# Fetching k and v as 112 rows and 16 more, and interleaving q, k and v with the weights

## The chip, the cores and the metric

The kernel runs on one core of a Trainium2 chip. A core has a matrix engine (TensorE, PE in the profile), a vector engine (VectorE, DVE), a scalar engine (ScalarE, ACT), GpSimd (POOL) and a sync engine (SyncE, SP) whose queue issues nearly all transfers here. The data is moved by 16 DMA engines. On-chip memory (SBUF) has 128 partitions; matmuls write to PSUM banks. The metric is the device time of one execution in microseconds, the median over several executions. Before the change it is 926.72 us (926.64 to 927.29 over 3 runs).

## What is computed

The kernel joins a linear attention block to a two-matrix feed-forward block. For each of 8 batches and 8 heads, with 576 positions and head size 64:

```python
kv = np.einsum('bhsd,bhse->bhde', k, v)
out = np.einsum('bhsd,bhde->bhse', q, kv)
rms = np.sqrt(np.mean(out * out, axis=-1, keepdims=True) + 1e-06)
x = (out / rms * g_norm)              # then (B,H,S,D) -> (B*S, H*D) = 4608 x 512
h = x @ w_in                          # 512 x 2048, float64 weights
sp = np.maximum(h, 0.0) + np.log1p(np.exp(-np.abs(h)))
y = (h * erf(sp)) @ w_out             # 2048 x 512
```

The feed-forward weights come as 64-bit floats, all else as 32-bit floats. What matters for the change is the first line. kv is a sum over the 576 positions, and TensorE sums over partitions, so the positions of k and v are spread over partitions in several chunks. In which chunk and partition a position lies makes no difference to the sum, as long as k and v agree.

## The kernel before

**Tiling.** The 4608 tokens are handled as nine groups of 512: the first 512 positions of each of the 8 batches (T = 0 to 7), and a ninth group of the 64 last positions of every batch (`x_last`). Heads are taken in pairs, four pairs (p = 0 to 3) to a batch. Pair i = 4T + p has one q tile, one k tile and one v tile in SBUF; the pools hold two of each kind (`bufs=2`).

**Stages.** Batch 0's attention is done alone at the start (to about 28 us) while the raw 64-bit weights begin to arrive. Groups 0 and 1 then run their feed-forward in a loop over n (32 steps of some 7 us, to about 250 us), the attention of the next batch running beside them in pieces. In group 0 the raw weights (`w_raw`, fetched by `load_w`, L213 and L218) are turned into 32-bit ones. In group 1 the 32-bit weights are cut into upper and lower parts: ACT writes the upper part (L596), VectorE the lower (L599, L602), and SP stores the three forms to DRAM (`w_in<-w_new`, `w_out<-w_new`, L672, 768 KB each). From group 2 on, the main loop runs steps m of about 23.8 us: four `hidden` products (x by w_in), and four `result` products (gates by w_out), each of 12 matmuls at L634. In every step all eight weight parts are read back from DRAM (`load_parts`, L773, 768 KB each), and one head pair of the next batch's attention is worked.

**One head pair of batches 1 to 7.** `load_pair(i)` fetches k and v of the pair two ahead, and `load_q` its q. `visit` applies kv to q, and forms the kv of the next pair (`kv_products`, L449, or L357 for the very first). `turn` transposes the next pair's q on VectorE (L318).

**How k and v lie.** For batches 1 to 7 the 576 positions are cut into C = 5 chunks. `rows, rest = divmod(S, C)` gives 115 rows and 1 over: partition r holds positions 5r to 5r+4 of each head, 1280 contiguous bytes, for r below 115 (L141), and the last position goes to partition 115, chunk 0, in a transfer of its own (L146, 0.5 KB). Batch 0 has 6 chunks of 96 rows and nothing over.

**How q lies.** Each q tile is fetched by eight transfers (L162) of 32 partitions each, in runs of 128 bytes.

**Order of the transfers.** There is no planner; the order is that of the program text. SP issues its transfers in that order. One waits, and all behind it, until its tile is free and until the transfer eight before it on SP has landed, since the transfers signal eight semaphores in turn. In a main-loop step, `fetch(place)` is called at eight places (0 to 3 after the four `hidden` products, 4 to 7 after the four `result` products) and issues weights by the list

```python
    FETCH = ("", "in", "in", "out", "in", "out", "in", "out out")
```

The attention's pieces are run at `places = (0, 2, 3, 5, 6, 8)`; in batches 3 to 7 the third piece, at place 3, holds `loads` and `turn`, so all twelve transfers of a pair (two for k, two for v, eight for q) are issued there in a row. In group 0 and 1's loop `loads` follows `visit`. The two first pairs of batch 1 are special: their k and v are requested in batch 0's loop (`i == 1`), the q of the first after that loop (`load_q(NP)`) and the q of the second at step n = 1.

Of the kernel before, what the change touches and what calls it, by code (L numbers as in the profile page):

```python
# [57 lines left out]
SQ = 32  # L58
# [3 lines left out]
def kernel(  # L62
# [10 lines left out]
    nc = tc.nc  # L73
    P = 128
    B, H, S, D = q.shape
# [4 lines left out]
    NP = H // 2  # L80
# [30 lines left out]
    exp_ln_table()  # L111


    q_sb, k_sb, v_sb = {}, {}, {}


    q_last = early.tile([P, 2, 2, D], FP32, name="q_last", bufs=1)
# [1 line left out]
    def chunks(T):  # L119

        return 6 if T == 0 else 5

    def load_pair(i, turned=True):
        T, p = divmod(i, NP)
        if T >= B:
            return
        pool = early if i in (2, 3) else kvp
        side = nc.scalar if i < 3 else nc.sync
        if T == 0:
            t = pool.tile([P, G if pool is early else S], FP32, name="q_sb", tag="q")  # L130
            t = q_sb[T, p] = t[:, 0:G].rearrange("p (j h d) -> p j h d", j=J, h=2)
            nc.sync.dma_start(
                out=t, in_=q[T, 2 * p : 2 * p + 2, 0:G, :].rearrange("h (p j) d -> p j h d", j=J)
            )
        for name, got, src in (("k", k_sb, k), ("v", v_sb, v)):
            C = chunks(T)
            rows, rest = divmod(S, C)
            assert rest < 2
            t = got[T, p] = pool.tile([rows + rest, 2, C, D], FP32, name=f"{name}_sb", tag=name)
            heads = src[T, 2 * p : 2 * p + 2]  # L140
            side.dma_start(  # L141
                out=t[:rows].rearrange("r h c d -> r h (c d)"),
                in_=heads[:, : S - rest].rearrange("h (r c) d -> r h (c d)", c=C),
            )
            if rest:
                side.dma_start(  # L146
                    out=t[rows:, :, 0], in_=heads[:, S - rest :].rearrange("h r d -> r h d")
                )
        if T > 0 and turned:
            load_q(i)  # L150

    def load_q(i):


        T, p = divmod(i, NP)
        t = q_sb[T, p] = kvp.tile([P, S], FP32, name="q_sb", tag="q")
        for n in range(P // SQ):
            h, w = divmod(n, D // SQ)
            to = t[n * SQ : n * SQ + SQ].rearrange("a (j b) -> a j b", b=SQ)
            for head, js in ((1 - h, slice(0, G // 2 // SQ)), (h, slice(G // 2 // SQ, S // SQ))):  # L160
                src = q[T, 2 * p + head, :, w * SQ : w * SQ + SQ]
                nc.sync.dma_start(  # L162
                    out=to[:, js], in_=src.rearrange("(j a) b -> a j b", a=SQ)[:, js]
                )

    def load_last(p):
        nc.sync.dma_start(
# [106 lines left out]
    def w_next(what):  # L274
        i = w_at[what]
        if i < len(w_order):
            w_at[what] = i + 1
            {"load": load_w, "split": w_split, "join": w_join}[what](*w_order[i][1:])
# [41 lines left out]
    def kv_products(T, p, at, crossed):  # L320


        ks, vs = (x.pop((T, p)) for x in (k_sb, v_sb))
        C = chunks(T)
        for c in range(C):
            for r in range(2):
                rows = (slice(0, D), slice(D, S // C + (c < S % C)))[r]
                for i in range(2):
                    yield partial(
                        nc.tensor.matmul,  # L330
                        at[rows_of[i], 1 - (r ^ i) if crossed else r, kv_cols],
                        lhsT=ks[rows, i, c],
                        rhs=vs[rows, i, c],
                        start=(c == 0),
                        stop=(c == C - 1),
                    )
# [29 lines left out]
    def attention(T, p, pools=None, in_parts=False):  # L366
# [31 lines left out]
        def products():  # L398

            kv_ps = st["kv"] = bank("kv_ps")  # L400
            ks, vs, qs = (x.pop((T, p)) for x in (k_sb, v_sb, q_sb))
            C = chunks(T)
            for c in range(C):
                rows = slice(0, S // C + (c < S % C))
                for i in range(2):
                    s = rows_of[i]
                    nc.tensor.matmul(
                        kv_ps[s, s],
                        lhsT=ks[rows, i, c],
                        rhs=vs[rows, i, c],  # L410
                        start=(c == 0),
                        stop=(c == C - 1),
                    )
            if p % 2 == 0:
                nc.tensor.transpose(kv_ps[:, q_tail], q_last[:, p // 2], ident)
            st["qT"] = square_tile("qT")
            for s in rows_of:
                nc.vector.tensor_copy(out=bd[s, s], in_=kv_ps[s, s])
            if p % 2 == 0:
                tails[T] = attp.tile([P, G], FP32, name="qT_last", tag="sq_lo")[:, 0:P]  # L420
                nc.vector.tensor_copy(out=tails[T], in_=kv_ps[:, q_tail])
            st["tail"] = tails[T][:, p % 2 * R : p % 2 * R + R]
            qt_ps = bank("qt_ps")
            for j in range(J):
                nc.tensor.transpose(qt_ps[:, j * P : j * P + P], qs[:, j], ident)
            nc.scalar.copy(st["qT"], qt_ps)
# [123 lines left out]
            split_lower()  # L550

        def loads():
            load_pair(T * NP + p + 2)

        if T == 0:
            return products, apply, halve, mean, norm
# [4 lines left out]
        first_ = (partial(prepare, T, p),) if (T, p) == (1, 0) else ()  # L561
        then_ = partial(turn, *then)
        if apart:
            pieces = (first_, (visit, halve, keep_tail), (loads, then_))
            return (*(partial(chain, *group) for group in pieces), mean, norm, *after)
        pieces = (first_, (visit, loads), (halve, keep_tail) if halves else (keep_tail,))
        return (*(partial(chain, *group) for group in pieces), mean, partial(chain, norm, then_), *after)
# [176 lines left out]
    for i in range(NP + 3):  # L744
        for piece, p in ((0, i), (1, i - 1), (4, i - 3), (3, i - 2)):
            if 0 <= p < NP:
                first[p][piece]()
        if i == 1:
            for _ in range(RAW - 2):
                w_next("load")  # L750
            load_pair(NP, turned=False)
            load_pair(NP + 1, turned=False)
        for what in w_rounds.get(i, ()):
            w_next(what)


    w_late.append(True)
    load_q(NP)
    first_batch, batches = FIRST * NB, NG * NB
    w_seq = {  # L760
        which: [(which, f) for _ in range(NG - FIRST) for f in range(FC)] for which in ("in", "out")
# [3 lines left out]
    def load_parts(which, n):  # L765


        pool = w_out_p if which == "out" and len(w_seq["out"]) > BATCH else w_in_p
        for _ in range(n):
            if w_seq[which]:  # L770
                key = w_seq[which].pop(0)
                t = pool.tile([P, 3, G], FP32, name=f"w_{which}_parts", tag="w")
                nc.sync.dma_start(out=t, in_=w_kept[key])  # L773
                w_now.setdefault(key, []).append(t)
# [47 lines left out]
    for n in range(FIRST * FC + 1):  # L822
# [58 lines left out]
        if T < FIRST:  # L881
            if n == whole:
                old_h = acc.tile([P, BATCH, G], FP32, name="h", tag="e")
            h = hs[n] = old_h[:, n - whole] if n >= whole else unit("h_sb")
            s = ss[n] = unit("s_sb")
            if n in plain:
                nc.scalar.copy(h, plain.pop(n))
            else:
                nc.scalar.activation(h, n_ps, AF.Copy, scale=SHIFT - 1.0)
                add(h, m_ps)  # L890
            if T == FIRST - 1:
                if f == 1:
                    x_both = wide.tile([P, KC, G], FP32R, name="x_both", tag="b")
                    for i in range(0, KC, 2):
                        both_only(x_high[:, i : i + 2], x_low[:, i : i + 2], x_both[:, i : i + 2])
                    x_forms[T] = x_high, x_low, x_both
                gates(done)
                for key in list(w_new):
                    w_lower(*key)
                for key in to_cut[f]:  # L900
                    w_upper(*key)
            nc.scalar.activation(s, h, AF.Softplus)
            if n == 0:
                w_next("split")
            if n == 1:
                load_q(NP + 1)
            for piece in steps[f][1]:
                piece()
            if f % BATCH == BATCH - 1:
                for i in range(n - BATCH + 1, n + 1):  # L910
                    nc.scalar.activation(ss[i], ss[i], AF.Erf)  # L911
                softplus_table()
            if T == FIRST - 1:
                load_parts("in", {FC - 3: 2, FC - 2: 1, FC - 1: 1}.get(f, 0))
# [9 lines left out]
        if T < FIRST:  # L924
            for piece in steps[f][2]:
                piece()
    for n in range(whole, FIRST * FC):
        gates(n)

# [46 lines left out]
    for m in range(first_batch, batches + 1):  # L976
# [10 lines left out]
        def piece():  # L987
            if todo:
                todo.pop(0)()
# [15 lines left out]
        def fetch(place):  # L1005
            for which in FETCH[place].split():
                load_parts(which, 1)


        pieces(0)  # L1010
# [100 lines left out]
```

## Time and profile before

| | |
|---|---|
| median time | 926.72 us |
| profiled span | 926.5 us |
| TensorE busy | 898.8 us (97%) |
| VectorE, ScalarE busy | 751.0 us (81%), 589.9 us (64%) |
| moved by DMA | 259.91 MB, mean 281 GB/s |
| weight parts read, per transfer | 768 KB (228 transfers) |
| k and v, per transfer | 287.5 KB and 0.5 KB (56 of each) |
| q of batches 1 to 7, per transfer | 32 or 40 KB (224 transfers) |

The profile's page gives busy time and share of each engine, a strip of 40 equal slices of the span in tenths, the costliest groups of instructions (line, engine, operation, tiles written and read, count, busy time, mean duration in ns, idle time of the engine just before and what ended it), and the DMA issues. "PEld" is the loading of TensorE's weights. "SPq" is SP's queue. Views of the same trace list the waits (who waited for whom: total us, times, longest), the chain of work that ended last, and the instructions of an engine in order of time (start, duration, engine, line, operation, tiles).

Times of transfers in the lists of an engine are those of issuing; the landing is seen in the chain or in the wait of a reader. The ends of matmuls are modelled, so neighbouring matmuls overlap in the trace.

### The profile page before, as it was taken

The page shows a single profiled execution, that of the slowest core. Times are in us where ns is not written, and L with a number is a line of the kernel's source. Part 1 is how long each engine was busy: PE and PEld are TensorE (multiplying, and loading weights), DVE is VectorE, ACT ScalarE, POOL GpSimd, SP SyncE. Part 2 cuts the span into 40 slices and gives each one's busy share as a digit, 9 for nine tenths or more (in the row PEclk, how much of TensorE's full clock was granted, in tenths as well). Part 3 has the DMA queues.
Part 4 walks back from the last instruction along what each step waited for, and adds up shares of the span by engine and source line. Part 5 has one row for each costly group of instructions (what it writes and reads, how often), then busy time and mean ns, then how long its engine had stood idle before and what let it go on. Part 6 is the DMA issues. An engine that isn't in the chain of part 4 may idle for free.

```text
span 926.5 us, 13591 instructions
## 1 busy us (share of the span) xinstructions
PE 898.8 (97%) x4990; PEld 668.6 (72%) x4990; DVE 751.0 (81%) x1088; ACT 589.9 (64%) x783; POOL 2.4 (0%) x10
## 2 busy tenths in 40 slices
PE   6999999988999999999999999999999999999998
PEld 4444445655587888778878888788878888888886
DVE  2799958888588888888888888888888888886777
ACT  3868766767675666656665666666666766665552
POOL 1000000000000000000000000000000000000000
PEclk9999999999999999999999999999999999999999
DMA  9767506698688888988898788887889788778871
GB/s 250 237 190 265 167 1 249 246 378 313 239 287 312 311 312 310 347 308 308 308 337 309 296 310 310 301 306 284 292 313 404 272 286 322 291 288 314 325 271 51
DMA packets 143210, 259.91 MB, mean 281 GB/s; under 512 B 78936, under 2 KB 101800, under 8 KB 143144
## 3 DMA queue, kind: packets, MB, share of 16 engines
q1 hardware_dynamic: 141432, 256.74, 75.7%
q10 hardware_dynamic: 1648, 2.29, 0.9%
q8 instruction: 40, 0.66, 0.3%
q14 instruction: 26, 0.21, 0.1%
q0 software_dynamic: 64, 0.00, 0.0%
HBM read 224.40 MB, written 34.60 MB: 280 GB/s over the span
## 4 chain that ended last, share of the span: by engine, by line
PE 76%; DMA 11%; DVE 6%; ACT 5%; issue 1%; SPq 1%; DVEq 0%; ACTq 0%
PE n_ps L634 41%; PE m_ps L634 20%; PE o_ps L690 6%; PE h_ps L874 4%; DMA w_out_parts<-w_out 4%; DMA w_in_parts<-w_in 2%; DMA w_in<-w_new 2%; DMA v_sb<-in_v_dram 1%; PE at_ps L449 1%; PE at_ps L435 1%; DMA w_raw<-in_moe_w_out_dram 1%; ACT s_sb L911 1%; DMA q_sb<-in_q_dram 1%; DVE h L612 1%; PE at_ps L496 1%
## 5 line engine op out<-in xcount | busy, mean ns | idle before, releaser
L634 PE MATMUL n_ps<-w_out_parts,g_forms 128*128 128x512 f32 x928 | 231.2, 391 | 1.7 <-DMA w_out_parts<-w_out 1.7
L634 PE MATMUL n_ps<-x_forms,w_in_parts 128*128 128x512 f32 x896 | 225.1, 393 | 3.2 <-DMA w_in_parts<-w_in 2.1
L634 PEld LDWEIGHTS n_ps<-w_out_parts,g_forms 128*128 128x128 f32 x928 | 172.4, 188 | 38.4 <-DMA w_out_parts<-w_out 3.3
L634 PEld LDWEIGHTS n_ps<-x_forms,w_in_parts 128*128 128x128 f32 x896 | 166.1, 188 | 41.1 <-ACT h L1024 3.2
L1039 ACT ACTIVATE s<-h 128x512 f32<-128x512 f32 x112 | 71.0, 634 | 180.9 <-DVE h L612 180.9
L612 DVE TENSOR_TENSOR h<-m_ps,h 128x512 f32<-128x512 f32 x116 | 79.9, 689 | 61.5 <-ACT h L1024 39.9
L634 PE MATMUL m_ps<-w_out_parts,g_forms 128*128 128x512 f32 (+1 forms) x468 | 124.3, 388 | 0.0
L634 PE MATMUL m_ps<-x_forms,w_in_parts 128*128 128x512 f32 x448 | 119.8, 389 | 0.0
L690 PE MATMUL o_ps<-w_out_sb,h_sb 128*128 128x512 f32 x224 | 101.5, 596 | 0.2 <-DVE h_sb L820 0.2
L634 PEld LDWEIGHTS m_ps<-w_out_parts,g_forms 128*128 128x128 f32 x468 | 87.5, 188 | 18.4
L634 PEld LDWEIGHTS m_ps<-x_forms,w_in_parts 128*128 128x128 f32 x448 | 84.1, 188 | 17.6
L612 DVE TENSOR_TENSOR e<-m_ps,e 128x512 f32<-128x512 f32 (+1 forms) x117 | 80.3, 687 | 14.1 <-PE m_ps L634 2.9
L1024 ACT ACTIVATE h<-n_ps 128x512 f32<-128x512 f32 x112 | 65.6, 585 | 16.6 <-PE n_ps L634 16.6
L690 PEld LDWEIGHTS o_ps<-w_out_sb,h_sb 128*128 128x128 f32 x224 | 41.3, 189 | 45.3 <-issue 42.8
L578 DVE SCALAR_TENSOR_TENSOR g_forms<-g_forms 128x1024 fp32r<-128x1024 f32 x58 | 71.1, 1225 | 2.0
L575 DVE TENSOR_TENSOR g_forms<-h,g_forms 128x1024 fp32r<-128x1024 f32 x58 | 70.6, 1217 | 1.2 <-ACT g_forms L572 1.1
L572 ACT ACTIVATE g_forms<-h 128x1024 fp32r<-128x1024 f32 x58 | 58.7, 1051 | 14.8 <-PE m_ps L634 10.9
L1071 DVE TENSOR_TENSOR h<-h,s 128x1024 f32<-128x1024 f32 x56 | 65.9, 1218 | 0.0
L874 PE MATMUL h_ps<-xT,w_in_sb 128*128 128x512 f32 x144 | 64.6, 594 | 0.0
L607 DVE SCALAR_TENSOR_TENSOR e<-n_ps,e 128x512 f32<-128x512 f32 x88 | 60.1, 683 | 1.5 <-PE n_ps L634 1.5
L109 ACT ACT_TABLE_LOAD x44 | 56.5, 1283 | 0.8
L874 PEld LDWEIGHTS h_ps<-xT,w_in_sb 128*128 128x128 f32 x144 | 27.1, 190 | 33.4 <-issue 31.6
(119 smaller groups left out, 990.7 us busy)
## 6 DMA issues: line engine op xcount, KB each, us to landing
w_out_parts<-w_out SPq DMA_DIRECT2D x116, 768.0 KB
w_in_parts<-w_in SPq DMA_DIRECT2D x112, 768.0 KB
w_in<-w_new SPq DMA_DIRECT2D x16, 768.0 KB
w_raw<-in_moe_w_in_dram SPq DMA_DIRECT2D x16, 512.0 KB
w_raw<-in_moe_w_out_dram SPq DMA_DIRECT2D x8, 1024.0 KB
out_dram<-e SPq DMA_DIRECT2D x32, 256.0 KB
k_sb<-in_k_dram SPq DMA_DIRECT2D x28, 287.5 KB
v_sb<-in_v_dram SPq DMA_DIRECT2D x28, 287.5 KB
```

Source lines behind the costliest of these rows:

```text
L109: nc.scalar.preload_act_table_set("softplus")
L572: nc.scalar.activation(high, x, AF.Copy, scale=1.0 + 2.0**-13)
L575: nc.vector.tensor_tensor(out=low, in0=x, in1=high.bitcast(FP32), op=ALU.subtract)
L578: nc.vector.scalar_tensor_tensor(out=both, in0=low.bitcast(FP32), scalar=SHIFT, in1=high.bitcast(FP32), op0=ALU.mult, op1=ALU.add,)
L607: nc.vector.scalar_tensor_tensor(out=out_, in0=ps, scalar=scale, in1=out_, op0=ALU.mult, op1=ALU.add)
L612: nc.vector.tensor_tensor(out=out_, in0=ps, in1=out_, op=ALU.add)
L634: nc.tensor.matmul(ps[:, cols], lhsT=weights(form, k), rhs=moving(form, k)[:, cols], start=(form == forms[0] and k == 0), stop=(form == fo ...
L690: nc.tensor.matmul(o_ps[j], lhsT=g[:, j * P : j * P + P], rhs=w_out_sb[:, f, :], start=(f == 0), stop=last,)
L874: nc.tensor.matmul(plain[i], lhsT=w_in_sb[:, i % FC, c], rhs=xT[T][:, c, :], start=(c == 0), stop=(c == KC - 1),)
L1024: nc.scalar.activation(h[:, i], n_ps, AF.Copy, scale=SHIFT - 1.0)
L1039: nc.scalar.activation(s[:, i], h[:, i], AF.Softplus)
L1071: nc.vector.tensor_tensor(out=part(h, half), in0=part(h, half), in1=part(s, half), op=ALU.mult)
```

## The change

There are two parts.

The first changes how k and v lie. A new `rows_in` gives 112 rows for the five chunks and 16 more for chunk 0: partition r below 112 holds positions 5r to 5r+4, and the last 16 positions go to partitions 112 to 127 of chunk 0. The kv products sum over 128 partitions in chunk 0 and over 112 in the others, rather than 116 and 115. It is meant to spread each transfer over more DMA engines.

The second changes when the transfers of k, v and q are issued. They are put on a list, `to_fetch`, and `fetch_some(n)` issues the next n of it: two after each raw weight in batch 0's loop, four at the end of each step in group 0 and 1's loop, two at each of the eight places of a main-loop step. In batches 3 to 7 `loads`, which allots the tiles and fills the list, moves from place 3 to place 0. The k and v of batch 1's first two pairs are still issued at once. It is meant to keep the weights from standing behind twelve transfers in a row.

```diff
+    def rows_in(T, c):
+        rows = S // chunks(T) // 16 * 16
+        return rows + (S - chunks(T) * rows if c == 0 else 0)
...
-            rows, rest = divmod(S, C)
-            assert rest < 2
+            rows, rest = rows_in(T, 1), rows_in(T, 0) - rows_in(T, 1)
...
-            side.dma_start(
-                out=t[:rows].rearrange("r h c d -> r h (c d)"),
-                in_=heads[:, : S - rest].rearrange("h (r c) d -> r h (c d)", c=C),
-            )
+            due_ = [
+                partial(
+                    side.dma_start,
+                    out=t[:rows].rearrange("r h c d -> r h (c d)"),
+                    in_=heads[:, : S - rest].rearrange("h (r c) d -> r h (c d)", c=C),
+                )
+            ]
...
+            if later:
+                to_fetch.extend(due_)
+            else:
+                for start in due_:
+                    start()
-        if T > 0 and turned:
+        if T > 0:
             load_q(i)
...
-                nc.sync.dma_start(
-                    out=to[:, js], in_=src.rearrange("(j a) b -> a j b", a=SQ)[:, js]
+                to_fetch.append(
+                    partial(
+                        nc.sync.dma_start,
+                        out=to[:, js],
+                        in_=src.rearrange("(j a) b -> a j b", a=SQ)[:, js],
+                    )
                 )
+    def fetch_some(n):
+        for due_ in to_fetch[:n]:
+            due_()
+        del to_fetch[:n]
...
-                rows = (slice(0, D), slice(D, S // C + (c < S % C)))[r]
+                rows = (slice(0, D), slice(D, rows_in(T, c)))[r]
...
-            load_pair(T * NP + p + 2)
+            load_pair(T * NP + p + 2, later=True)
...
-            pieces = (first_, (visit, halve, keep_tail), (loads, then_))
+            pieces = ((loads,), (visit, halve, keep_tail), (then_,))
...
-            load_pair(NP, turned=False)
-            load_pair(NP + 1, turned=False)
+            load_pair(NP)
+            load_pair(NP + 1)
         for what in w_rounds.get(i, ()):
             w_next(what)
+            if what == "load":
+                fetch_some(2)
 
     w_late.append(True)
-    load_q(NP)
...
-            if n == 1:
-                load_q(NP + 1)
...
         if T < FIRST:
             for piece in steps[f][2]:
                 piece()
+            fetch_some(4)
...
             for which in FETCH[place].split():
                 load_parts(which, 1)
+            fetch_some(2)
```

More of the change, by code (lines that the diff above doesn't have):

```diff
@@ L111 @@
     exp_ln_table()
-    q_sb, k_sb, v_sb = {}, {}, {}
+    q_sb, k_sb, v_sb, to_fetch = {}, {}, {}, []
     q_last = early.tile([P, 2, 2, D], FP32, name="q_last", bufs=1)
@@ L121, in chunks, with load_pair @@
         return 6 if T == 0 else 5
-    def load_pair(i, turned=True):
+    def rows_in(T, c):
+        rows = S // chunks(T) // 16 * 16
+        return rows + (S - chunks(T) * rows if c == 0 else 0)
+    def load_pair(i, later=False):
         T, p = divmod(i, NP)
@@ L136, in load_pair @@
             C = chunks(T)
-            rows, rest = divmod(S, C)
-            assert rest < 2
+            rows, rest = rows_in(T, 1), rows_in(T, 0) - rows_in(T, 1)
             t = got[T, p] = pool.tile([rows + rest, 2, C, D], FP32, name=f"{name}_sb", tag=name)
             heads = src[T, 2 * p : 2 * p + 2]
-            side.dma_start(
-                out=t[:rows].rearrange("r h c d -> r h (c d)"),
-                in_=heads[:, : S - rest].rearrange("h (r c) d -> r h (c d)", c=C),
-            )
-            if rest:
-                side.dma_start(
-                    out=t[rows:, :, 0], in_=heads[:, S - rest :].rearrange("h r d -> r h d")
-                )
-        if T > 0 and turned:
+            due_ = [
[5 more added lines that the diff above has]
+            ]
+            if rest:
+                due_.append(
+                    partial(
+                        side.dma_start,
+                        out=t[rows:, :, 0],
+                        in_=heads[:, S - rest :].rearrange("h r d -> r h d"),
+                    )
+                )
+            if later:
[4 more added lines that the diff above has]
+        if T > 0:
             load_q(i)
@@ L161, in load_q @@
                 src = q[T, 2 * p + head, :, w * SQ : w * SQ + SQ]
-                nc.sync.dma_start(
-                    out=to[:, js], in_=src.rearrange("(j a) b -> a j b", a=SQ)[:, js]
-                )
+                to_fetch.append(
+                    partial(
+                        nc.sync.dma_start,
+                        out=to[:, js],
+                        in_=src.rearrange("(j a) b -> a j b", a=SQ)[:, js],
+                    )
+                )
+    def fetch_some(n):
+        for due_ in to_fetch[:n]:
+            due_()
+        del to_fetch[:n]
     def load_last(p):
@@ L403, in products @@
             for c in range(C):
-                rows = slice(0, S // C + (c < S % C))
+                rows = slice(0, S // C)
                 for i in range(2):
```

## The prediction

> **What bounds the kernel now.** I read the page first: its busy rows, the slices, the matmul groups.
>
> ```profile
> span 926.5 us, 13591 instructions
> PE 898.8 (97%) x4990; PEld 668.6 (72%) x4990; DVE 751.0 (81%) x1088; ACT 589.9 (64%) x783; POOL 2.4 (0%) x10
> ...
> DMA  9767506698688888988898788887889788778871
> ...
> L634 PE MATMUL n_ps<-w_out_parts,g_forms 128*128 128x512 f32 x928 | 231.2, 391 | 1.7 <-DMA w_out_parts<-w_out 1.7
> L634 PE MATMUL n_ps<-x_forms,w_in_parts 128*128 128x512 f32 x896 | 225.1, 393 | 3.2 <-DMA w_in_parts<-w_in 2.1
> ```
>
> TensorE is the bound: 28 us idle in all. The DMA engines are busy 80 to 90% on average from 225 us on. A time can only be won where TensorE stands still, so the second view is the list of TensorE's own waits.
>
> ```profile
> PE kv_ps L407 <- DMA v_sb<-in_v_dram: 7.2, 2, 5.9
> PE n_ps L634 <- ACT h_sb L889: 3.4, 1, 3.4
> PE n_ps L634 <- ACT h L889: 2.8, 1, 2.8
> PE n_ps L634 <- DMA w_in_parts<-w_in: 2.1, 2, 1.7
> PE at_ps L435 <- DVE qT L318: 2.0, 1, 2.0
> PE n_ps L634 <- DMA w_out_parts<-w_out: 1.7, 2, 0.9
> ```
>
> Columns: total, times, longest. The 7.2 us are batch 0 (96-row k and v from 0 to 15 us), which the change leaves alone. Still open to it: 2.0 (first q of batch 1), 3.4 and 2.8 (two late ACT evacuations, at 193 and 224 us), 3.8 (late weights). Where nothing waits, the 12 matmuls of one product start 2.72 us apart from the next 12; the excess over this at the four weight waits (386, 483, 599, 672 us) is 0.92, 1.07, 1.86 and 0.60, so 4.4 us. Together with the others at most about 14 us hang on this change.
>
> Then the SP queue in time, over one step of the main loop:
>
> ```profile
> 351.57 3.04 SPq L773 DMA_DIRECT2D w_in_parts<-w_in  x2
> 354.66 0.33 SPq L141 DMA_DIRECT2D k_sb<-in_k_dram  x1
> 355.04 1.45 SPq L146 DMA_DIRECT2D k_sb<-in_k_dram  x1
> 356.53 0.44 SPq L141 DMA_DIRECT2D v_sb<-in_v_dram  x1
> 357.01 4.93 SPq L146 DMA_DIRECT2D v_sb<-in_v_dram  x1
> 362.05 7.83 SPq L162 DMA_DIRECT2D q_sb<-in_q_dram  x8
> 369.92 0.46 SPq L773 DMA_DIRECT2D w_out_parts<-w_out  x1
> ```
>
> The twelve transfers of one head pair hold the queue from 354.66 to 369.92, 15.3 us, in which no weight can be issued; six weights follow within 8 us. In the chain that ended last, weights issued at 374.77 land after 12.33 us, at 471.41 after 12.59, and at 590.87 after 10.12. TensorE then waits at 386, 483 and 599.
>
> **What the Trainium skill says.** "DMA: Bandwidth & Descriptors", section "Why a DMA increments its semaphore by 16 and not by 1": a transfer goes over the largest k up to 16 that divides the outermost sizes of both sides, and each engine used posts one increment. So 115 rows use 5 engines, the leftover row (outer size 2) uses 2, while 112 and 16 rows use 16. The trace agrees: SP's 679 transfers have 9,464 four-byte completion packets, and 56 x 5 + 56 x 2 + 567 x 16 = 9,464. The same page, "Queues, rings and completion order": each engine consumes its ring in order, and a DMA uses the lowest-numbered k. So all k and v lie on the same five rings, and every weight waits on them there. No view shows single engines; the 4.93 us of the tiny v transfer above fits a full ring. "Perfetto Trace Analysis", "Identifying the Most-Contended Engine", says that matmul busy time misjudges distance to the roofline since matmuls are pipelined; the trace agrees (12 x 391 ns is 4.7 us, in 2.72 us), hence starts, not busy time, above.
>
> **How full the five engines are.** The step from 525.07 to 548.88 us has a mean DMA share of 0.83, so 19.8 us per engine in 23.8. Its k and v are 460 packets of 1280 bytes at 56 ns (packet records), 25.8 us of engine time: 1.6 per engine if spread over 16, 5.2 on five. The five carry 19.8 - 1.6 + 5.2 = 23.4 us of 23.8, an estimate: full. The other eleven carry 18.2.
>
> **The change, part by part.**
>
> *112 rows and 16 more.* All engines carry 19.8 us (0.83). That this is enough is seen at the end of the run: from 749 to 794 us no k, v or q is fetched, the share is 0.81 to 0.87, and TensorE is busy without a gap. The 16-row transfers have 32 packets of 256 bytes at 19 ns: 0.6 us over 16 engines, nothing. SP's issues stay twelve per pair. The kv products change from 51 and 52 lower rows to 48 and 64; these take 218 to 230 ns now whether 51, 52 or 64 rows, so nothing.
>
> *Two at a time.* Between two weights stand at most two small transfers, about 0.9 us at the q median of 0.45 us, in place of a burst of 7 to 15 us. Weights go out when their buffers come free. What is queued behind a small transfer on SP is the next weight or store. A transfer waits for the one eight before it on SP (they signal eight semaphores in turn), so a small one may stand behind a weight that has not landed: SP waits for this now too (L162 for w_in_parts, 23.1 us over 21 times). Cost between 0, when weights land in under 8 us, and about 0.5 us a step; I take 0, as the five full rings that make for 10 to 12 us are gone.
>
> *Fetches at place 0 rather than 3 in batches 3 to 7.* Buffers of k, v and q are then already free (their readers ran in the step before), so no new wait; needed a step (23.8 us) later. Hidden.
>
> *q of batch 1's first pair, between the raw weights.* Now its eight transfers are issued from 36.51 us, after the last raw weight; VectorE waits 3.9 us for them and TensorE 2.0. After, four go out behind the raw weights near 27 us and four by about 37, so q is there before bd_kv at 43.8. Between 50 and 150 us TensorE is 100% busy, so the gain stays: 2.0. The raw weights land later by this one pair's q at most: 2304 packets of 128 bytes at 12.5 ns over 16 engines, 1.8 us. The raw weight that lands last now, at 45.9, is used at 48.4, so this is hidden.
>
> *Batch 1's loop (150 to 260 us).* ACT's erf at 192.6 is late because the split weight's buffer is stored late: issued 185.32, landed 4.72 later, ACT waiting 1.44 + 1.36 us. The rings of the five engines carry 5.2 us of k and v from 173.7, where 1.6 would do, and SP's burst ends only at 184.7. I take 1.8 of the 3.6 us there, bounds 0 and 3.6. The gap at 224 stays: there ACT waits 1.31 us for TensorE itself at 220.0, whatever the stores do.
>
> *Main loop.* The 4.4 us of late weights go. Small gaps at 285 and 406 us (0.9, 0.4) follow ACT and VectorE and stay.
>
> Sum: 2.0 + 1.8 + 4.4 = 8.2; 926.7 - 8.2 = 918.5.
>
> **Rivals.**
>
> *All stalls go, 912 to 914 (0.10).* The 224 us gap and those at 285 and 406 follow too: 14 us. For it: ACT's 2.15 us wait for a store at 218. Against: the TensorE wait just after it.
>
> *Part only, 922 to 925 (0.10).* The start's 2.0 us and up to half of 4.4; the weights are late from the out stores at the batch ends (1 MB; 93% share from 370 to 380 us), not from k and v. For it: three of the four weight waits (386, 483, 672) follow stores. Against: the one at 599, the longest, follows none, and from 749 to 771 us four stores go out at a share of 0.87 with no TensorE wait.
>
> *No change, 925 to 928 (0.08).* Late weights are rare now (four), and as many new ones may come at other places; the start's gain is then taken up by ACT before 193 us, where TensorE waits for it anyway.
>
> *Slower, 930 to 936 (0.08).* The wait on the transfer eight before moves from the burst to before each weight: 18 steps with fetches x 0.5 us = 9 us, less the 2 at the start, so 933. For it: transfers in flight are then mixed with 768 KB weights. Against: eight transfers in flight hold some three weights, and one weight is 128 packets of 6144 bytes at 249 ns over 16 engines, 2.0 us: three are 6 us, while eight of a step's twenty transfers span 8/20 of 23.8, 9.5 us.
>
> **How the numbers follow.** Forecast, 915 to 922: 0.64. With the rivals, faster by over 0.2% is 0.64 + 0.10 + 0.10 = 0.84, same 0.08, slower 0.08. The range leaves out the last two and a little of the first rival: 913.5 to 925.
>
> **What would show it.** Right: no TensorE wait for w_in_parts or w_out_parts; completion packets up to 679 x 16 = 10,864; no leftover-row issue over about 1 us; weights landing in under 8 us; no wait of qT for q at 47 us; the gap at 193 halved. Wrong: new SP waits ahead of the weights (L773 on a q, k or v), ACT waiting longer for the stores between 150 and 260 us, or weight waits at batch ends that stay.

## The result and the profile after

The changed kernel takes 918.03 us (917.64 to 918.55) against 927.0 for the kernel before in the same runs: a ratio of 0.9898, interval 0.988 to 0.9916. The forecast was 918.5. The total was right, and so was the mechanism in the main loop, but two terms of the sum were not: the stages ahead of the main loop gave more than forecast and the main loop less. That these two cancelled is luck.

The page of the changed kernel:

```profile
span 915.9 us, 13573 instructions
...
PE 896.3 (98%) x4990; PEld 668.1 (73%) x4990; DVE 750.1 (82%) x1088; ACT 589.2 (64%) x783; POOL 2.4 (0%) x10
...
L659 PE MATMUL n_ps<-w_out_parts,g_forms 128*128 128x512 f32 x928 | 230.5, 390 | 0.3 <-DMA w_out_parts<-w_out 0.3
L659 PE MATMUL n_ps<-x_forms,w_in_parts 128*128 128x512 f32 x896 | 224.4, 392 | 0.0
...
w_out_parts<-w_out SPq DMA_DIRECT2D x116, 768.0 KB, 7.3
w_in_parts<-w_in SPq DMA_DIRECT2D x112, 768.0 KB, 6.9
```

TensorE does the same work with 19.6 us idle instead of 27.7. The idle time ahead of the weight products fell from 1.7 and 3.2 us to 0.3 and 0.0. The last two lines give a weight's median from issue to landing, about 7 us. The chain before showed late weights only, at 10 to 12.6 us. Counted from the semaphore records of both traces, the weights of the main loop (250 to 760 us) have medians of 10.0 (w_in) and 8.6 us (w_out) before and 7.0 and 7.5 after. Over 8 us took 106 of 172 before and still 49 of 175 after, so the sign "landing in under 8 us" came true for the median and not for every weight.

Where the time was won is seen in the first and last start of the products with w_in in the main loop, before and after:

```profile
L634 PE MATMUL n_ps<-x_forms,w_in_parts x896: 387/389/791, 251.4 to 898.9; 128*128 128x512 f32 x180
L659 PE MATMUL n_ps<-x_forms,w_in_parts x896: 387/389/790, 243.8 to 888.2; 128*128 128x512 f32 x180
```

7.6 us are won before the main loop starts and 3.1 in it. (This is one profiled execution of each kernel. The one of the kernel before took 928.31 us, above its median, so these add up to more than the 9.0 between the medians.)

TensorE's waits in the changed kernel (total, times, longest):

```profile
PE kv_ps L432 <- DMA v_sb<-in_v_dram: 8.0, 3, 5.8
PE at_ps L521 <- DVE bd_kv L366: 2.1, 3, 0.9
...
PE n_ps L659 <- ACT h_sb L915: 0.9, 1, 0.9
PE at_ps L521 <- DVE x_last L482: 0.9, 1, 0.9
PE n_ps L659 <- DMA w_out_parts<-w_out: 0.3, 1, 0.3
```

The waits for w_in_parts, for qT and for the evacuation `h` are gone. The second and fourth lines are new: the mean matmuls of a pair now wait for VectorE's copies, at four batch ends (424, 520, 616 and 712 us). They had no place in the forecast. One sign that the prediction had named for being wrong did come: the weights' line now waits on SP for k and v.

```profile
SPq L799 <- DMA v_sb<-in_v_dram: 8.7, 16, 0.7
SPq L799 <- DMA k_sb<-in_k_dram: 8.6, 12, 1.2
```

The small transfers, too, wait longer for weights than before (86.9 us in all at L188, against 44.5 at L146 and L162). With at most 1.2 us at a time ahead of a weight, TensorE's list shows no loss from this.

The SP queue in one main-loop step of the changed kernel (start, duration, engine, line, operation, tiles, count):

```profile
340.04 0.93 SPq L188 DMA_DIRECT2D k_sb<-in_k_dram  x2
343.08 0.34 SPq L799 DMA_DIRECT2D w_in_parts<-w_in  x1
343.47 0.93 SPq L188 DMA_DIRECT2D v_sb<-in_v_dram  x2
345.80 0.34 SPq L799 DMA_DIRECT2D w_in_parts<-w_in  x1
346.24 0.87 SPq L188 DMA_DIRECT2D q_sb<-in_q_dram  x2
347.17 0.45 SPq L799 DMA_DIRECT2D w_out_parts<-w_out  x1
```

No burst, and the 4.93 us that a leftover-row transfer could hold the queue have become 0.93 for two transfers. The four-byte completion packets number 10,864, which is 679 x 16: every transfer of SP now uses 16 engines. The packet records also show it without a rule. Of the time from 250 to 760 us in which any 1280-byte packet of k or v is open, five are open at once for 57% before, and never more than 8; after, up to 21 are. (The counts run a little over the number of engines, since packets overlap: in the kernel on one engine, below, up to 2 are open.) A pair's k and v were in flight together before, issued 2 us apart and some 12.6 us on their way, so five at once, and not ten, also says that they shared their engines.

### The profile page after: what moved, and what is told of

The parts are those of the page before. It is cut to its first block, busy times and chain, and to the rows that moved or that the text cites. A ratio compares the mean times of both kernels' runs of the same rounds, so it can differ in the third digit from the quotient of the medians.

```text
span 915.9 us, 13573 instructions
## 1 busy us (share of the span) xinstructions
PE 896.3 (98%) x4990; PEld 668.1 (73%) x4990; DVE 750.1 (82%) x1088; ACT 589.2 (64%) x783; POOL 2.4 (0%) x10
## 3 DMA queue, kind: packets, MB, share of 16 engines
q1 hardware_dynamic: 144176, 256.75, 82.1%
## 4 chain that ended last, share of the span: by engine, by line
PE 72%; DVE 10%; DMA 8%; ACT 6%; issue 2%; SPq 1%; DVEq 0%; ACTq 0%
PE n_ps L659 38%; PE m_ps L659 19%; PE h_ps L900 6%; PE o_ps L715 5%; DMA q_sb<-in_q_dram 3%; DVE e L637 1%; PE at_ps L474 1%; PE at_ps L460 1%; DMA w_out_parts<-w_out 1%; DVE h L1097 1%; DVE h L637 1%; DVE e L632 1%; ACT s_sb L935 1%; DMA q_last<-in_q_dram 1%; DMA out_dram<-e 1%
## 5 line engine op out<-in xcount | busy, mean ns | idle before, releaser
L1065 ACT ACTIVATE s<-h 128x512 f32<-128x512 f32 x112 | 70.9, 633 | 181.0 <-DVE h L637 181.0
L632 DVE SCALAR_TENSOR_TENSOR e<-n_ps,e 128x512 f32<-128x512 f32 x88 | 60.1, 682 | 1.0 <-PE n_ps L659 0.9
```

Of the source, the lines that this page charges most:

```text
L632: nc.vector.scalar_tensor_tensor(out=out_, in0=ps, scalar=scale, in1=out_, op0=ALU.mult, op1=ALU.add)
L1065: nc.scalar.activation(s[:, i], h[:, i], AF.Softplus)
```

## The experiments

The theory: k and v on five engines fill these, and every weight waits in their rings; the rows cure it. The first rival: the burst of twelve on the SP queue makes the weights late, and the order cures it.

**The rows alone.** The kernel before with

```diff
-            rows, rest = divmod(S, C)
+            rows, rest = rows_in(T, 1), rows_in(T, 0) - rows_in(T, 1)
```

and the matching rows in the products; order and burst as before.

> The kernel before with the 112 + 16 rows alone; the twelve transfers of a pair stay in one burst. My theory (five full rings make the weights late; spreading them is the larger part): the late weights of the main loop and most of the gap near 193 us go, the wait for q at 47 us stays: 920 to 922 us. Rival (the burst on the SP queue makes the weights late, the number of engines matters little): 925 to 927 us.

Measured: 918.27 us (917.52 to 919.68), ratio 0.989 (0.9869 to 0.9912). All of the gain, within the ranges, and more than I had given it. The burst is still there, as the SP queue of this kernel shows:

```profile
346.96 0.42 SPq L145 DMA_DIRECT2D k_sb<-in_k_dram  x1
347.44 0.45 SPq L150 DMA_DIRECT2D k_sb<-in_k_dram  x1
347.93 0.43 SPq L145 DMA_DIRECT2D v_sb<-in_v_dram  x1
348.40 0.46 SPq L150 DMA_DIRECT2D v_sb<-in_v_dram  x1
348.96 8.99 SPq L166 DMA_DIRECT2D q_sb<-in_q_dram  x8
357.99 0.46 SPq L777 DMA_DIRECT2D w_out_parts<-w_out  x1
```

For 11.0 us no weight is issued, and yet TensorE waits for a main-loop weight once, for 1.0 us. So the burst was not what made the weights of the main loop late.

**The order alone.** The changed kernel with

```diff
-        rows = S // chunks(T) // 16 * 16
+        rows = S // chunks(T)
```

> The changed kernel with rows 115 + 1 again, so only the order of the transfers is changed. My theory: the start's 2.0 us are won, the rings of five engines stay full, so weights still come late: 922 to 925 us, or worse where a weight now waits behind k and v that were issued earlier. Rival (the burst is the cause): 917 to 920 us, as the whole change.

Measured: 941.79 us, ratio 1.0134 (1.0111 to 1.0157): slower than the kernel before, which took 928.52 us in the same runs, and 17 us past my figure, by the clause that I had put behind it. The same line as above, for this kernel:

```profile
L659 PE MATMUL n_ps<-x_forms,w_in_parts x896: 387/389/792, 244.8 to 908.8; 128*128 128x512 f32 x180
```

The main loop starts 6.6 us earlier than before, and all of that and 9.9 us more are lost in it. Ahead of the main loop the order alone thus wins nearly as much as the rows alone (243.8 us, so 7.6): there either part of the change is nearly enough, and the rival is not refuted. In the main loop the rows help, and the order alone does harm. (The profiled execution took 938.23 us and is the fastest of the six.)

What SP waits for in this kernel's main loop (250 to 760 us), and TensorE in the same stretch:

```profile
SPq L799 <- DMA v_sb<-in_v_dram: 51.1, 18, 3.3
SPq L799 <- PE m_ps L659: 43.5, 22, 9.9
SPq L799 <- DMA k_sb<-in_k_dram: 27.7, 17, 2.1
```

```profile
PE n_ps L659 <- DMA w_in_parts<-w_in: 8.7, 7, 2.6
PE n_ps L659 <- ACT s L1065: 3.5, 1, 3.5
PE n_ps L659 <- DMA w_out_parts<-w_out: 2.7, 4, 1.1
```

L799 is the weights' line. A weight is now the transfer eight after a large k or v and cannot be issued until that has landed on its five full rings: 78.8 us of waiting, where the kernel before had its q transfers wait there instead (L162 for v_sb and k_sb, 36.9 us in the same stretch). Part of the loss is TensorE's clock: the trace grants half speed for 3.41 us from 384 us, 1.5 us after a wait for a weight had ended, and for 6.83 us from 483 us, towards the end of the 3.5 us wait in the list. By the starts of the products in these stretches this costs some 4.5 us. One stretch of it, in the same kernel (busy times of PE, PEld, DVE, ACT and POOL, then the granted clock, 0.50, the DMA share and GB/s):

```profile
484.00:489.40 5.40, 5.26 (x13) 4.18 (x13) 0.13 (x1) 0.71 (x2) 0.00 (x0) 0.50 1.04 358
```

The Trainium skill, "TensorE: Matmul & The Clock Gate", Part 1, has two states of the clock, full and half, and the half one after an idle window of some 3.4 us. The trace agrees on the two states, and the two stretches last once and twice that time; on the idle time not quite, since an idle gap of 2.23 us at 380 was followed by half speed and one of 2.62 us at 680 was not.

**The order, shifted off the eight.** As the last kernel, but

```diff
-            fetch_some(2)
+            fetch_some((4, 2, 3, 3, 2, 2, 2, 2)[place])
```

in the main loop, so that q and not a weight is eight behind k and v.

> Rows 115 + 1 in the new order, but 4, 2, 3, 3 small transfers at the first four places of a main-loop step, so that the transfers eight after a large k or v are those of q, not weights. If the new order loses on five engines because weights wait on SP for the k or v eight before: L799's waits for k_sb and v_sb go, and the time falls to 925 to 931 us. If it loses because the full rings delay the weights in whatever order: 936 to 944 us.

Measured: 928.81 us, ratio 1.0006 (0.9988 to 1.0024). In its main loop the waits have moved to the line of the small transfers:

```profile
SPq L188 <- DMA v_sb<-in_v_dram: 45.2, 18, 3.3
SPq L188 <- DMA k_sb<-in_k_dram: 37.2, 18, 3.0
```

SP waits as long as before (82.4 us against 78.8), but now it is q that stands there. So most of the new order's loss on uneven engines depends on which transfer stands eight behind k and v. TensorE's waits for weights fell only from 11.4 to 8.9 us; the 3.5 us wait and the half-speed stretches in the main loop are gone altogether. (The run also issues k and v at one place rather than two, which was not tried apart.) In total the order then gains nothing on five engines: its main loop starts at 245.6 us, 5.8 earlier than before, and gives that back.

**More and fewer engines.** The changed kernel's order with other rows:

```diff
-        rows = S // chunks(T) // 16 * 16
+        rows = 96 if T == 0 else 114
```

and 113 in its place. By the divisors 114 + 6 rows lie on 6 engines, and of 113 + 11 rows the 113 on one.

> The changed kernel with 114 rows and 6 more: by the rule of divisors six engines for the large k and v transfers. Theory of the full engines: the six carry 18.2 + 25.8/6 = 22.5 us of a 23.8 us step against 23.4 on five, so still too full where stores are added: between the changed kernel and the one with five engines and the new order (941.8), 922 to 938 us. If only something special of 115 + 1 (the one-row transfers on two engines) were the cause: about 918 us.

> The changed kernel with 113 rows and 11 more, so that by the rule of divisors the large k and v transfers of batches 1 to 7 lie on one engine. It is a larger dose of the suspected cost with the same order and bytes. My theory: that engine carries some 18 us of a main-loop step's work and 448 packets x 56 ns = 25 us more, 43 us in a step of 23.8; 18 steps with fetches lose near 20 us each, the group-1 loop some more: 1200 to 1320 us. If engines don't matter: 918 to 922 us.

Measured: 928.85 us on six (0.9993, 0.9974 to 1.0012), 1388.27 us on one (1.4948, 1.4896 to 1.4999). With the two kernels above this is a series in the same order of transfers; beside the engines only the leftover rows differ (16, 6, 1 and 11):

| engines of k and v | estimated load of a step on the fullest, us of 23.8 | time, us |
|---|---|---|
| 16 | 19.8 | 918.0 |
| 6 | 22.5 | 928.9 |
| 5 | 23.4 | 941.8 |
| 1 | 43 | 1388.3 |

The step from six engines to five, 13 us, is as large as what the shifted order wins back on five. So the series mixes the load with the wait on the transfer eight before, and its slope is not the cost of an engine.

In the kernel on one engine the completion packets number 9,744 = 567 x 16 + 56 x 1 + 56 x 11, and from 250 to 760 us the 1280-byte packets are open one at a time (94% of the time that any is, never over 2). So it is one, and 11 for the leftover rows. Its main loop takes 166 to 169 us for a batch of four steps, some 42 a step, where 43 was the estimate (113 rows make 452 packets and not 448, which changes nothing here). TensorE's longest wait in it, and the SP queue in one step:

```profile
PE n_ps L659 <- DMA w_in_parts<-w_in: 250.4, 44, 12.0
```

```profile
605.79 13.99 SPq L188 DMA_DIRECT2D k_sb<-in_k_dram  x2
619.88 0.35 SPq L799 DMA_DIRECT2D w_in_parts<-w_in  x1
620.27 12.88 SPq L188 DMA_DIRECT2D v_sb<-in_v_dram  x2
```

Here the weights are late because SP is held while it issues k and v: once issued, a weight lands after 8.0 to 8.4 us in the median, which is no longer than before. On five engines both things happen: the leftover-row transfers hold SP (a median of 1.3 us for k and 2.4 for v), and weights take longer to land. The even rows end both, and no run tells apart how much each is worth.

The total overshot my range: the main loop lost 341 us, as reckoned (18 x 20 = 360), and the stages ahead of it 131, which I had put too low. The granted clock averaged 0.854 in this run; TensorE is idle for 26 of the 80 us from 600 to 680, so the clock is more likely a result of the waits than a cause of the time.

**The early q alone undone.** The changed kernel without the two fetches after each raw weight; the first pair's q goes out after batch 0's loop:

```diff
     w_late.append(True)
+    fetch_some(8)
```

> The changed kernel, but the q of batch 1's first pair is issued after batch 0's loop as before. My theory: VectorE's wait for q and TensorE's gap at 46 us come back, TensorE is full from there to 190 us, so the 2.0 us stay: 919.5 to 920.5 us. Rival (ACT and the stores take them up before 193 us): 918 us.

Measured: 918.83 us (918.17 to 919.38). Between the two expectations: at most 0.8 us, not 2.0, and the ranges overlap; the ratios to the kernel before, 0.9893 and 0.9898, show no cost. TensorE's gap at 46 us comes back as 0.58 us rather than 2.15, and in the kernel with the rows alone, whose q is as late in the program as before, it is 0.28. So the place in the program had a small part in it. SP does not issue this q earlier in these kernels: its first transfer goes out at 36.80 and 35.51 us, before at 36.51. By the semaphore records the eighth goes out when the raw weight eight before it has landed, and that weight took 9.8 us before (36.09 to 45.88) and 8.2 and 8.0 us here (to 44.56 and 43.08).

**The new wait.** At a batch's end the changed kernel's TensorE waits for VectorE's copies of the visit. I moved that visit one product forward:

```diff
-            places = (0, 0 if T + 1 == B else 2, 2 if T + 1 == B else 3, 4, 5, 5, 6)
+            places = (0, 0 if T + 1 == B else 1, 2, 4, 5, 5, 6)
```

> The changed kernel with the visit of each batch's last pair one product earlier (place 1 rather than 2, turn at 2 rather than 3). In the changed kernel TensorE waits 0.7 to 1.1 us at four batch ends (424, 520, 616 and 712 us) for VectorE's copies of the visit before the mean matmuls. If VectorE's place in its own order is the cause: these four gaps close, 914.5 to 916 us. If VectorE is simply full there, the gap moves to another wait: 917.5 to 918.5 us.

Measured: 917.3 us (917.09 to 918.15), between the two expectations. The waits for `bd_kv` and `x_last` are gone from TensorE's list, but 0.4 us for `e` (L632) is new, and gaps of 0.2 to 0.6 us stand at later steps.

**All four side by side**, on the same chip:

> The changed kernel, beside the next three on the same chip, to compare them with one another: 918.0 us. If the new order adds to the rows, it is below the rows alone by 0.5 us or more; if the order is idle once the engines are even, within 0.3 us of it.

> The rows alone, in the order of the kernel before: 918.3 us. Order idle: within 0.3 us of the changed kernel. Order of worth: 0.5 us or more above it.

> The changed kernel with the earlier visit at batch ends: 917.3 us. If it is a true gain: 0.5 to 1 us under the changed kernel of the same call. If the earlier figure was chance: the same.

> The rows alone, in the order of the kernel before, with the earlier visit at batch ends. If VectorE's place at batch ends is the limit whatever the order of transfers: the four gaps before the mean matmuls close here too, 917.3 to 917.7 us, the best with the least change. If the burst of twelve then makes weights late again: 918 to 920 us.

| kernel | time, us | range |
|---|---|---|
| before | 928.13 | 927.64 to 930.76 |
| rows alone | 918.68 | 918.32 to 918.92 |
| the change | 917.96 | 917.66 to 918.46 |
| rows and earlier visit, old order | 917.44 | 917.18 to 918.47 |
| the change and earlier visit | 917.19 | 916.99 to 917.88 |

The rows bring 9.4 of the 10.2 us. The order adds 0.7 and the earlier visit 0.8 (1.2 in the old order), at the edge of what the ranges tell apart. Both together are the fastest that was run, but the rows and the earlier visit in the old order are within 0.3 us of them, and no weight is late there for the burst. The earlier visit closes gaps of 3.6 us and wins 0.8: from one batch's first softplus (L1065) to the next one's it is 96.0 us with it and without, so most of the gain is given back within the batch. What sets these 96.0 us, where four steps of 23.8 are 95.2, was not settled.

## Why the prediction was right, and where it was not

*Five full engines.* Five shared engines are shown: the completion packets fit the divisors, the packets open at once say the same, and the rows alone bring nearly the whole gain. (That the lowest-numbered engines are taken stands in the section on the increments of 16, not in the one on queues and rings that the prediction names.) "Full" is not shown. The 23.4 us of 23.8 are an estimate from packet times, and these overlap: the mean share is over 1 in the stretch above (1.04), and 1.05 from 380 to 390 us in the changed kernel, where TensorE is busy throughout. And "every weight waits on them there" is one of two ways in which the five engines cost time; the other is that SP is held.

*Main loop, 4.4 us.* Right in the cause, too large as a term: the four weight waits are down to 0.3 us of idle time, but the main loop gives 3.1 us in all. The small gaps at 285 and 406 us, which I let stay since they followed ACT and VectorE (the trace names ACT for both), went too (1.3 us), and four waits for VectorE that I had not seen came (1.08, 0.73, 0.73 and 1.04). The step that failed is "Small gaps ... stay", and the list of rivals lacked a new bound: while TensorE waited for weights, VectorE caught up. The rows alone bring the same four waits (2.5 us of idle time), so they come from weights that are on time and not from the order.

*Batch 1's loop, 1.8 us.* The term was much too small: 5.2 us. The gap at 193 us fell from 3.59 to 1.10 (by the starts, less the usual distance), so 2.5. The step "the gap at 224 stays: there ACT waits 1.31 us for TensorE itself" was wrong: it fell from 2.96 to 0.25. ACT's row of the kernel before, and SP's:

```profile
218.05 0.64 ACT L596 ACTIVATE w_new<-w_out_sb 128x512 fp32r<-128x512 f32 x1 [2.15 <-DMA w_out<-w_new]
220.00 0.64 ACT L596 ACTIVATE w_new<-w_in_sb 128x512 fp32r<-128x512 f32 x1 [1.31 <-PE n_ps L634]
```

```profile
208.08 6.56 SPq L162 DMA_DIRECT2D q_sb<-in_q_dram  x8
214.75 0.39 SPq L672 DMA_DIRECT2D w_out<-w_new  x1
215.25 0.36 SPq L672 DMA_DIRECT2D w_in<-w_new  x1
```

The matmul named as the releaser ended at 219.97. The store issued at 215.25, behind the burst, landed at 219.91 by its semaphore records. In the kernel with the rows alone, where it is issued at 207.68:

```profile
210.57 0.63 ACT L600 ACTIVATE w_new<-w_out_sb 128x512 fp32r<-128x512 f32 x1
212.49 0.63 ACT L600 ACTIVATE w_new<-w_in_sb 128x512 fp32r<-128x512 f32 x1 [1.28 <-DMA w_in<-w_new]
```

The store leaves earlier, its landing is named as the releaser, and TensorE's wait after it is 0.4 us where it was 2.8. Two releasers had ended together, the view named one, and I took it. What frees the store is not the five engines alone: the order alone, on five engines, closes most of these gaps too.

*The start, 2.0 us.* The gap closed as forecast, but the early q was not needed for it: with the rows alone 0.28 of 2.15 us are left, and undoing the early q costs at most 0.8 us. What the even rows changed there is the landing of the raw weight that q's last transfer waits for.

*Two at a time, taken as 0.* Right on even engines (0.7 us gained, at the edge of the ranges), and for the reason named, "the five full rings ... are gone". The rival "slower" was real where they are not: its mechanism, a wait on the transfer eight before, is what the order alone ran into, at 13 us over the kernel before.

*The sum.* 2.0 + 1.8 + 4.4 = 8.2 was forecast. By gaps of TensorE: about 2.2 at 46 us, 2.5 and 2.7 in batch 1's loop, some 4.1 for the weights and 1.3 beside them, less 3.6 new. That is 9.2. It should be held against the spans of the same two profiled executions, which differ by 10.6; the rest was not traced, except that 0.6 of it lies ahead of 45 us, by the starts of the same matmuls in both traces. The medians differ by 9.0. So the total of 8.2 came close because batch 1's loop gave 3.4 more than its term and the new waits took 3.6 away.

## What to carry to other kernels

Look at how many engines a transfer's row count gives it: 115 rows and 1 move the same bytes as 112 and 16, and cost 9 us of 927 here, since weights and SP's queue wait behind five engines. A mean DMA share of 0.83 can hide engines at an estimated 0.98. Even the engines first and reorder after: on uneven ones the better-looking order lost 13 us, because each transfer waits for the one eight before it, and weights stood there.

## What the hardware showed that I had not expected

The packets got slower in the mean, while the medians stayed (55 ns for 1280 bytes, 234 ns for 6144). For 6144 bytes this goes with the new order and not with the even engines; the last column is the main queue's share of the engines' time:

| kernel | 1280 bytes, mean ns | 6144 bytes, mean ns | share |
|---|---|---|---|
| before | 56 | 249 | 75.7% |
| rows alone | 71 | 252 | 78.8% |
| the change | 66 | 268 | 82.1% |
| order alone | 70 | 275 | 82.4% |

The change and the order alone have nearly the same share, and in the one the weights are on time, in the other late. So the mean share says little of whether weights arrive in time.
